# Two decode layers on one core: loading the second layer's first chunks in parts

## The chip, the cores and the metric

The kernel runs on one core of a Trainium2 chip. The metric is the device time of one execution in microseconds (us). It was measured in three runs; the median counts. A further execution was recorded by the hardware profiler.

## The reference, cut to what matters

Two identical layers are applied to four tokens (one per batch entry) of width 512: attention over a cache of 8192 positions, then a SwiGLU feed-forward network (FFN). All data are bfloat16. Both layers use the same weights and the same caches.

```python
# A_x (4,1,512); k_cache, v_cache (4, 8, 8192, 128); wq (512, 4096); wo (4096, 512)
# w_gate, w_up (512, 1792); w_down (1792, 512)
def attention(x):                       # 32 query heads, 8 kv heads, 4 queries for each kv head
    q = (x @ wq) -> (4, 32, 1, 128)
    scores = q . k * 128 ** -0.5
    return (softmax(scores) . v) -> (4, 1, 4096) @ wo

def ffn(x):
    return (silu(x @ w_gate) * (x @ w_up)) @ w_down

for layer in range(2):
    x = x + attention(layernorm(x))
    x = x + ffn(layernorm(x))
```

The K and V caches are 67 MB each and each layer needs both; the weights are some 14 MB.

## The kernel before

**Units and chunks.** A *unit* is one kv head of one batch entry; there are 32 (`unit_order`). The K cache of a unit is a *chunk* of 2 MB, 16 KB for each of the 128 SBUF partitions, and so is its V cache. A chunk has eight blocks of 2 KB per partition, which are the grain of the synchronisation: the resources `s6.0` to `s6.7` are the blocks of slot 6.

**Slots.** SBUF holds eight slots of one chunk each (`NSLOT`). The K and V chunks of layer 1's last three units stay in slots 0 to 5 (`kept`), and layer 2 begins with these three units (29, 30, 31) and goes on with units 0 to 28. So layer 2 loads six chunks fewer. Here *k0* is the kept K chunk of unit 29 and *k1* that of unit 30.

**FFN weights.** They are loaded at the end of each layer into slots 6 and 7 and a stretch behind them. `wg_sb` (w_gate) takes blocks 0 to 6 of slot 6; the last of the four row blocks of w_up (`wu_sb[FR]`) takes block 7 of slot 6 and the beginning of slot 7; w_down follows in slot 7. The other three row blocks of w_up have a place of their own. `at_w` lists the resources that the FFN's matmuls read.

**Loads.** All loads are issued by SP, in the order of the list `items`. `pump()` walks through the list as long as a slot is free; `finished()` frees a slot when the scores (K) or the weighted sum (V) of a unit have been written out, and calls `pump()`. `T.dma` (line 93 issues it) makes SP wait first until all readers of the destination's resources are done (line 63), so SP stands still at a load whose place is still being read, and everything behind it waits too. The 16 DMA engines work through what SP has issued.

At the boundary between the layers, the first K chunk goes to slot 6 and the second to slot 7; `pump()` at the end of `ffn` issues both. The first waits for the matmuls of w_gate and w_up, since both lie in slot 6, the second for those of w_down. The third chunk (a V chunk, `half_it`) takes k0's slot in two halves: `half(0)` after block 3 of k0 has been used, `half(1)` after block 7. The fourth takes k1's slot when k1 is done. From there on chunks take the slots of V 29, K 31, V 30 and so on.

**Compute.** DVE transposes each K block (line 394), PE computes its scores (line 414), DVE, ACT and PE make the softmax (lines 420 to 450), PE multiplies by V (line 495) and, for each four units, by wo (line 522). The kept K chunks are already transposed. The FFN's matmuls are on line 593 (w_gate, then w_up) and 610 (w_down, in three parts). The order of the work on each engine is the order in which the Python program emits it; `keys`, `values`, `line` and `drain` interleave the stages by fixed costs.

Of the kernel before, what the change touches and what calls it, by code (L numbers as in the profile page):

```python
# [103 lines left out]
def bass_interleave_layers__gqa_block_cached__swiglu_ffn__decode_kernel(  # L104
# [12 lines left out]
    B, _, D = A_x.shape  # L117
    _, G, S, Dh = A_k_cache.shape
    HqDh = A_wq.shape[1]
    Hq = HqDh // Dh  # L120
    F = B_w_gate.shape[1]
    REP = Hq // G
    P = 128
    assert Dh == P and B * Hq == P and D % P == 0 and F % P == 0 and B == 4
    KT = D // P
    FO = F // P
    XB = KT * B
    TT = S // P
    TB = 8
    NB = TT // TB  # L130
# [7 lines left out]
    NQ = 4  # L138
    NSLOT = 8
    NKEEP = 6  # L140
# [5 lines left out]
    with ExitStack() as es:  # L146
# [3 lines left out]
        SL = TT * Dh  # L150
        FR = KT - 1
        kvf = sb("kvf", [P, NSLOT * SL + FR * F], BF16)
        kv = kvf[:, 0:NSLOT * SL].rearrange("p (s w) -> p s w", s=NSLOT)
        f0 = NKEEP * SL
        wg_sb = kvf[:, f0:f0 + KT * F].rearrange("p (k f) -> p k f", k=KT)
        wu_sb = [kvf[:, NSLOT * SL + k * F:NSLOT * SL + (k + 1) * F] for k in range(FR)]
        wu_sb.append(kvf[:, f0 + KT * F:f0 + (KT + 1) * F])
        f1 = f0 + (KT + 1) * F
# [1 line left out]
        wd_sb = kvf[:, f1:f1 + FO * D].rearrange("p (f n) -> p f n", f=FO)  # L160
        places = [f"s{s}.{q}" for s in range(NKEEP, NSLOT) for q in range(NB)]
        room = lambda a, b: places[(a - f0) // (TB * Dh):(b - 1 - f0) // (TB * Dh) + 1]
        at_w = {"wg": room(f0, f0 + KT * F) + ["wg"], "wu": room(f0 + KT * F, f1) + ["wu", "wu3"],
                "wd": room(f1, f1 + FO * D)}
        WD = ((0, 6), (6, 12), (12, 14))
        wq_sb = sb("wq_sb", [P, KT, HqDh], BF16)
        wo_sb = sb("wo_sb", [P, Hq, D], BF16)
# [34 lines left out]
        n = 2 * FO * B  # L202
# [10 lines left out]
        def bank_bf(k):  # L213
# [6 lines left out]
        sem = lambda name: es.enter_context(nc.semaphore(name))  # L220
        engines = {"pe": nc.tensor, "act": nc.scalar, "dve": nc.vector, "pool": nc.gpsimd, "sp": nc.sync}
        prog = {n: sem(f"prog_{n}") for n in engines}
        sem_s = [sem(f"sem_s{i}") for i in range(NSLOT)]
        sem_l = [sem(f"sem_l{q}") for q in range(NQ)]
        sem_x = sem("sem_x")
        sem_w = {n: [sem(f"sem_{n}{i}") for i in range(c)]
                 for n, c in (("wq", KT), ("wo", 4), ("wg", 1), ("wu", 2), ("wd", 3))}
        sem_out = sem("sem_out")
        es.enter_context(nc.Block())
        T = _Sync(engines, prog)  # L230
# [25 lines left out]
        def unit_gb(u):  # L256
            return u // B, u % B
# [3 lines left out]
        unit_order = [list(range(NU)), list(range(NU - NRES, NU)) + list(range(NU - NRES))]  # L261
# [10 lines left out]
        items = []  # L272
# [5 lines left out]
        ends = [i for i, it in enumerate(items) if it[0] == "wd"]  # L278
        split = {items[e - 3] for e in ends}

        half_it = items[ends[0] + 3]
        halves = []
        issued = [0]
        free = list(range(NSLOT))
        slot_of = {}
# [1 line left out]
        def load_weight(name, i=0):  # L287
            if name == "wq":
                T.dma("sp", wq_sb[:, i, :], A_wq[i * P:(i + 1) * P, :], sem_w["wq"][i], writes=[f"wq{i}"])
            elif name == "wo":  # L290
                n = Hq // 4
                T.dma("sp", wo_sb[:, i * n:(i + 1) * n, :],
                      A_wo[i * n * Dh:(i + 1) * n * Dh, :].rearrange("(h p) n -> p h n", p=P),
                      sem_w["wo"][i], writes=[f"wo{i}"])
            elif name == "wg":
                T.dma("sp", wg_sb, B_w_gate.rearrange("(kt p) f -> p kt f", p=P), sem_w["wg"][0], writes=places + ["wg"])
            elif name == "wu":
                if i == 0:
                    T.dma("sp", kvf[:, NSLOT * SL:].rearrange("p (k f) -> p k f", k=FR),
                          B_w_up[0:FR * P, :].rearrange("(kt p) f -> p kt f", p=P), sem_w["wu"][0], writes=["wu"])  # L300
                T.dma("sp", wu_sb[FR], B_w_up[FR * P:, :], sem_w["wu"][1], writes=["wu3"])
            else:

                for j, (a, b) in enumerate(WD):
                    T.dma("sp", wd_sb[:, a:b, :].rearrange("p (m e) n -> p m (e n)", e=2),
                          B_w_down[a * P:b * P, :].rearrange("(m p e) n -> p m (e n)", p=P, e=2), sem_w["wd"][j],
                          writes=[f"wd{j}"])

        def pump():
            while issued[0] < len(items):  # L310
                n = issued[0]
                it = items[n]
                if it[0][0] == "w":
                    if it[0] == "wg":
                        if not {NKEEP, NKEEP + 1} <= set(free):
                            return
                        free[:] = [s for s in free if s < NKEEP]
                    load_weight(*it)
                    issued[0] += 1
                    continue  # L320

                late = any(e - 10 < n < e for e in ends)
                fit = [s for s in free if s < NKEEP or not late]
                if not fit:
                    return
                s = fit[0] if late else max(fit, key=lambda s: s >= NKEEP)
                free.remove(s)
                kind, L, u = it
                slot_of[it] = s
                g, b = unit_gb(u)  # L330
                cache = A_k_cache if kind == "K" else A_v_cache
                src = cache[b, g, :, :].rearrange("(p t) d -> p (t d)", p=P)
                if it in split:
                    w = TT * Dh // NQ
                    n8 = NB // NQ
                    for q in range(NQ):
                        T.dma("sp", kv[:, s, q * w:(q + 1) * w], src[:, q * w:(q + 1) * w], sem_l[q],
                              writes=[f"s{s}.{q * n8 + k}" for k in range(n8)])
                else:
                    T.dma("sp", kv[:, s, :], src, sem_s[s], writes=[f"s{s}.{q}" for q in range(NB)])  # L340
                issued[0] += 1

        def half(i):
            kind, L, u = half_it
            g, b = unit_gb(u)
            s = slot_of[half_it]
            w = SL // 2
            src = (A_k_cache if kind == "K" else A_v_cache)[b, g, :, :].rearrange("(p t) d -> p (t d)", p=P)
            T.dma("sp", kv[:, s, i * w:(i + 1) * w], src[:, i * w:(i + 1) * w], sem_l[i],
                  writes=[f"s{s}.{i * NB // 2 + k}" for k in range(NB // 2)])  # L350

        def half_done(it):
            if it == ("K", 1, unit_order[1][0]):
                assert items[issued[0]] == half_it and it in slot_of
                slot_of[half_it] = slot_of[it]
                issued[0] += 1
                half(0)

        def finished(it):
            kind, L, u = it  # L360
            if (kind, 1, u) in kept and L == 0:
                slot_of[kind, 1, u] = slot_of[it]
                if kind == "K":
                    turned.update((1, u, q) for q in range(NB))
            elif it == ("K", 1, unit_order[1][0]):
                half(1)
                pump()
            else:
                free.append(slot_of[it])
                pump()  # L370

# [92 lines left out]
        def keys(L, u):  # L464
            def block(q):
                if q == 0:
                    place_q(u)
                scores(L, u, q)
                if q == NB // 2 - 1:
                    half_done(("K", L, u))  # L470
                if q == NB - 1:
                    finished(("K", L, u))
                    for gap, fn in ((0.0, max_p), (1.0, max_t), (0.9, exps), (1.0, turn_p), (0.3, total)):
                        line.append([gap, u, lambda fn=fn: fn(u)])

            for q in range(NB):
                if (L, u, q) not in turned:
                    turn(L, u, q)
                blocks.append((0.65, lambda q=q: block(q)))
                drain(LAG)  # L480
# [100 lines left out]
        def ffn(last):  # L581
# [5 lines left out]
            for (w_sb, wname, bk) in (([wg_sb[:, k, :] for k in range(KT)], "wg", gb), (wu_sb, "wu", ub)):  # L587
                for fo in range(FO):
                    if bk == gb and fo == FO // 2:
                        deviation(zero_sb, "zero")  # L590
                    f = fo // 2 * 2 * P + fo % 2
                    for kt in range(KT):
                        T.op("pe", lambda e: e.matmul(bank(bk)[:, fo * B:(fo + 1) * B],
                                                      lhsT=w_sb[kt][:, f:f + 2 * P - 1:2],
                                                      rhs=xn[:, kt * B:(kt + 1) * B],
                                                      start=(kt == 0), stop=(kt == KT - 1)),
                             reads=at_w[wname] + ["xn"], writes=[f"pb{bk}"], sig=(fo == FO - 1 and kt == KT - 1))
            T.op("dve", lambda e: e.tensor_tensor(fb(gr), fb(gT), rb, ALU.mult),
                 reads=[f"pb{gb}", "rstd"], writes=["gr"])
            T.op("act", lambda e: e.activation(eg, gr, ACTF.Exp, scale=-1.0), reads=["gr"], writes=["eg"])  # L600
# [6 lines left out]
            for j, (a, b) in enumerate(WD):  # L607
# [6 lines left out]
                             reads=["hT", f"wd{j}"] + at_w["wd"], writes=[f"pb{dn[j]}"], sig=(fo == b - 1))  # L614
                if j < len(WD) - 1:
                    add_to_x(dn[j])
            free.extend((NKEEP, NKEEP + 1))
            pump()
            if last:
                T.op("dve", lambda e: e.tensor_tensor(xoT[:], xT[:], bank(dn[-1])[:, 0:XB], ALU.add),  # L620
# [72 lines left out]
```

## Time and profile before

| | us |
|---|---|
| median of three runs | 668.08 |
| lowest and highest | 667.45, 668.77 |
| the profiled execution | 667.48 |
| its span on the engines | 665.2 |
| PE busy | 495.9 (75%) |
| DVE busy | 380.9 (57%) |
| DMA queue q1, share of 16 engines | 98.4% |
| moved | 274.96 MB, mean 413 GB/s |

All times in the profile count from the start of the span. A "releaser" is the instruction or DMA that ended a wait. The chain is found by going back from the last instruction to what released each one. Busy shares are averages over stages with different limits.

### The profile page before, as it was taken

The page shows a single profiled execution, that of the slowest core. Times are in us where ns is not written, and L with a number is a line of the kernel's source. Part 1 is how long each engine was busy: PE and PEld are TensorE (multiplying, and loading weights), DVE is VectorE, ACT ScalarE, POOL GpSimd, SP SyncE. Part 2 cuts the span into 40 slices and gives each one's busy share as a digit, 9 for nine tenths or more (in the row PEclk, how much of TensorE's full clock was granted, in tenths as well). Part 3 has the DMA queues.
Part 4 walks back from the last instruction along what each step waited for, and adds up shares of the span by engine and source line. Part 5 has one row for each costly group of instructions (what it writes and reads, how often), then busy time and mean ns, then how long its engine had stood idle before and what let it go on. Part 6 is the DMA issues. An engine that isn't in the chain of part 4 may idle for free.

```text
span 665.2 us, 16774 instructions
## 1 busy us (share of the span) xinstructions
PE 495.9 (75%) x7400; PEld 396.5 (60%) x7400; DVE 380.9 (57%) x879; ACT 89.9 (14%) x331; POOL 19.8 (3%) x75
## 2 busy tenths in 40 slices
PE   1765777877867857876775999877777786887686
PEld 1554565655745646665565878755665565665575
DVE  1645565655765655665641279675566465576572
ACT  1010111101101101111110112110110111110120
POOL 0000000000000000000000000000000000000000
PEclk9887788687878788788885979877878868788885
DMA  8999999999999999999998999999999999999996
GB/s 358 416 408 407 420 429 424 426 426 429 425 427 425 427 429 424 428 422 428 427 404 341 345 426 428 426 425 426 429 424 429 426 427 426 424 429 426 426 415 234
DMA packets 27032, 274.96 MB, mean 413 GB/s; under 512 B 2376, under 2 KB 6480, under 8 KB 10960
## 3 DMA queue, kind: packets, MB, share of 16 engines
q1 hardware_dynamic: 26960, 273.89, 98.4%
q8 instruction: 58, 0.95, 0.6%
q14 instruction: 14, 0.11, 0.0%
HBM read 273.88 MB, written 0.00 MB: 412 GB/s over the span
## 4 chain that ended last, share of the span: by engine, by line
DMA 68%; PE 16%; SPq 10%; DVE 3%; issue 2%; POOL 0%; ACT 0%; DVEq 0%; POOLq 0%
DMA kvf<-in_A_k_cache_dram 63%; PE ps L414 11%; SPq L93 10%; DMA kvf<-in_B_w_down_dram 5%; PE ps L495 3%; DVE kvf L394 1%; PE ps L436 1%; PE ps L424 1%; DVE pT L445 0%; PE ps L560 0%; DVE mx L420 0%; PE ps L448 0%; PE ps L610 0%; DVE rl L450 0%; PE ps L574 0%
## 5 line engine op out<-in xcount | busy, mean ns | idle before, releaser
L394 DVE STREAM_TRANSPOSE kvf<-kvf 128x512 f32<-128x512 f32 x488 | 313.2, 677 | 199.4 <-DMA kvf<-in_A_k_cache_dram 199.4
L414 PE MATMUL ps<-kvf,zq 128*128 128x256 bf16 x2048 | 330.6, 318 | 9.5 <-DVE kvf L394 6.5
L414 PEld LDWEIGHTS ps<-kvf,zq 128*128 128x128 bf16 x2048 | 215.3, 113 | 69.7 <-DVE kvf L394 9.8
L495 PE MATMUL ps<-pT,kvf 128*128 128x32 bf16 x4096 | 124.1, 179 | 37.1 <-DVE rl L450 35.1
L495 PEld LDWEIGHTS ps<-pT,kvf 128*128 128x128 bf16 x4096 | 120.8, 97 | 45.1 <-issue 39.8
L424 PE MATMUL ps<-identf,mx 128*1 128x128 f32 x64 | 19.5, 304 | 92.8 <-DVE mx L420 92.8
L430 ACT ACTIVATE pb<-m 1x128 f32<-1x128 f32 x64 | 19.7, 308 | 399.6 <-DVE m L427 399.6
L424 PEld LDWEIGHTS ps<-identf,mx 128*1 128x1 f32 x64 | 5.2, 81 | 96.7 <-DVE mx L420 96.6
L405 POOL TENSOR_TENSOR zq<-scr,quad 128x64 bf16<-128x64 bf16 x64 | 18.7, 292 | 618.3 <-PE ps L414 550.8
L436 PEld LDWEIGHTS ps<-onesf,pb 1*128 1x128 f32 x128 | 24.4, 237 | 19.6 <-issue 17.9
L445 DVE STREAM_TRANSPOSE pT<-pb 128x256 bf16<-128x256 bf16 x64 | 26.9, 421 | 12.6 <-ACT pb L440 12.0
L440 ACT ACTIVATE pb<-ps,nm 128x256 bf16<-128x256 f32 x64 | 30.4, 475 | 2.1
L420 DVE TENSOR_REDUCE mx<-ps 128x1 f32<-128x256 f32 x64 | 25.1, 393 | 8.6 <-PE ps L414 8.6
L436 PE MATMUL ps<-onesf,pb 1*128 1x1 f32 x128 | 29.9, 300 | 0.1
L439 ACT ACTIVATE nm<-ps 128x1 f32<-128x1 f32 x64 | 11.0, 171 | 134.3 <-PE ps L436 134.3
L448 PEld LDWEIGHTS ps<-rsm,onesf 128*128 128x128 f32 x128 | 20.7, 203 | 2.6 <-ACT rsm L442 0.6
L448 PE MATMUL ps<-rsm,onesf 128*128 128x4 f32 x128 | 19.8, 225 | 0.5 <-ACT rsm L442 0.5
L427 DVE TENSOR_REDUCE m<-ps 1x4 f32<-1x128 f32 x64 | 15.9, 249 | 7.1 <-PE ps L424 6.6
L442 ACT ACTIVATE rsm<-head,rs 128x4 f32<-128x4 f32 x64 | 19.0, 297 | 2.1
L503 DVE TENSOR_TENSOR oT<-ps,rl 128x4 bf16<-128x4 f32 x64 | 7.9, 123 | 10.4 <-PE ps L495 10.1
L560 PE MATMUL ps<-xn,wq_sb 128*128 128x4 bf16 x256 | 7.5, 165 | 8.1 <-DMA wq_sb<-in_A_wq_dram 8.1
L522 PEld LDWEIGHTS ps<-oT,wo_sb 128*128 128x128 bf16 x256 | 8.8, 105 | 6.8 <-DVE oT L503 5.2
(55 smaller groups left out, 91.4 us busy)
## 6 DMA issues: line engine op xcount, KB each, us to landing
kvf<-in_A_k_cache_dram SPq DMA_DIRECT2D x61, 2048.0 KB, 31.0
kvf<-in_A_v_cache_dram SPq DMA_DIRECT2D x58, 2048.0 KB, 32.2
wq_sb<-in_A_wq_dram SPq DMA_DIRECT2D x4, 1024.0 KB, 8.1
wo_sb<-in_A_wo_dram SPq DMA_DIRECT2D x4, 1024.0 KB, 19.4
kvf<-in_A_v_cache_dram SPq DMA_DIRECT2D x8, 512.0 KB, 18.8
kvf<-in_B_w_gate_dram SPq DMA_DIRECT2D x2, 1792.0 KB, 23.4
kvf<-in_B_w_down_dram SPq DMA_DIRECT2D x4, 768.0 KB, 16.4
kvf<-in_A_v_cache_dram SPq DMA_DIRECT2D x2, 1024.0 KB, 7.2
```

The costliest lines, as they stand in the source:

```text
L93: ins = self.eng[engname].dma_start(out_ap, in_ap)
L394: T.op("dve", lambda e: e.transpose(w, w), reads=[f"s{s}.{q}"], writes=[f"s{s}.{q}"])
L414: T.op("pe", lambda e: e.matmul(bank(bk)[:, 0:SW], lhsT=zq[:, c, z0:z0 + P], rhs=w[:, :, c // 2, :, c % 2], start=(q == 0 and c == 0), sto ...
L420: T.op("dve", lambda e: e.tensor_reduce(mx[:], bank(bk)[:, 0:SW], AX.X, ALU.max), reads=[f"pb{bk}"], writes=["mx"])
L424: T.op("pe", lambda e: e.matmul(bank(STEP)[0:1, 0:P], lhsT=mx[:], rhs=identf[:], is_transpose=True, start=True, stop=True), reads=["mx", " ...
L430: T.op("act", lambda e: e.activation(mrow.rearrange("p (x h) -> p x h", h=REP), m4[:].unsqueeze(1).to_broadcast([1, QB, REP]), ACTF.Copy), ...
L436: T.op("pe", lambda e: e.matmul(bank(STEP)[:, 0:1], lhsT=mrow, rhs=onesf[0:1, :], start=True, stop=True), reads=["pb", "onesf"], writes=[f ...
L440: T.op("act", lambda e: e.activation(pb[:], bank(bk)[:, 0:SW], ACTF.Exp, bias=nm[:], accum_out=rs[:]), reads=[f"pb{bk}", "nm"], writes=["p ...
L442: T.op("act", lambda e: e.activation(rsm[:], head[:], ACTF.Copy, scale=rs[:]), reads=["head", "rs"], writes=["rsm"])
L445: T.op("dve", lambda e: e.transpose(pT[:, turn_of[u], 0:SW], pb[:]), reads=["pb"], writes=[f"pT{turn_of[u]}"])
L448: T.op("pe", lambda e: e.matmul(bank(TOT)[:, 0:REP], lhsT=ones, rhs=rsm[:], start=True, stop=True), reads=["rsm", "onesf"], writes=[f"pb{T ...
L495: T.op("pe", lambda e: e.matmul(bank(bk)[:, 0:WIDE], lhsT=kv[:, s, t * Dh:(t + 1) * Dh], rhs=pT[:, turn_of[u], c0:c0 + WIDE], start=(t == ...
```

## The change

The first chunk of layer 2 (slot 6) loads in two parts: blocks 0 to 6 once w_gate's matmuls are emitted, block 7 once w_up's are. The third chunk loads in four quarters, after blocks 1, 3, 5 and 7 of k0, and the fourth in two halves, after blocks 3 and 7 of k1. The second is as before. Each part has a semaphore of its own (`sem_p`). In layer 1 alone, the last row block of w_up is loaded by five DMAs of 8, 4, 2, 2 and 112 rows in the place of one of 128 rows. `load` replaces `half` and the issuing code in `pump`; `load_part` replaces `half_done`.

```diff
--- before.py
+++ after.py
@@ -160,8 +160,9 @@
         wd_sb = kvf[:, f1:f1 + FO * D].rearrange("p (f n) -> p f n", f=FO)
         places = [f"s{s}.{q}" for s in range(NKEEP, NSLOT) for q in range(NB)]
         room = lambda a, b: places[(a - f0) // (TB * Dh):(b - 1 - f0) // (TB * Dh) + 1]
-        at_w = {"wg": room(f0, f0 + KT * F) + ["wg"], "wu": room(f0 + KT * F, f1) + ["wu", "wu3"],
+        at_w = {"wg": room(f0, f0 + KT * F) + ["wg"], "wu": room(f0 + KT * F, f1) + ["wu"] + [f"wu3{j}" for j in range(5)],
                 "wd": room(f1, f1 + FO * D)}
+        WU3 = ((0, 8), (8, 12), (12, 14), (14, 16), (16, 128))
         WD = ((0, 6), (6, 12), (12, 14))
         wq_sb = sb("wq_sb", [P, KT, HqDh], BF16)
         wo_sb = sb("wo_sb", [P, Hq, D], BF16)
@@ -222,9 +223,10 @@
         prog = {n: sem(f"prog_{n}") for n in engines}
         sem_s = [sem(f"sem_s{i}") for i in range(NSLOT)]
         sem_l = [sem(f"sem_l{q}") for q in range(NQ)]
+        sem_p = [sem(f"sem_p{i}") for i in range(8)]
         sem_x = sem("sem_x")
         sem_w = {n: [sem(f"sem_{n}{i}") for i in range(c)]
-                 for n, c in (("wq", KT), ("wo", 4), ("wg", 1), ("wu", 2), ("wd", 3))}
+                 for n, c in (("wq", KT), ("wo", 4), ("wg", 1), ("wu", 6), ("wd", 3))}
         sem_out = sem("sem_out")
         es.enter_context(nc.Block())
         T = _Sync(engines, prog)
@@ -278,8 +280,14 @@
         ends = [i for i, it in enumerate(items) if it[0] == "wd"]
         split = {items[e - 3] for e in ends}
 
-        half_it = items[ends[0] + 3]
-        halves = []
+
+        parts = {}
+        k0, k1 = (("K", 1, u) for u in unit_order[1][:2])
+        for it, ps_ in ((items[ends[0] + 1], (("wg", 0, 7), ("wu", 7, 8))),
+                        (items[ends[0] + 3], [((k0, q + 1), q, q + 2) for q in range(0, NB, 2)]),
+                        (items[ends[0] + 4], [((k1, q + 3), q, q + 4) for q in range(0, NB, 4)])):
+            for ev, a, b in ps_:
+                parts[ev] = (it, a, b, sem_p[len(parts)])
         issued = [0]
         free = list(range(NSLOT))
         slot_of = {}
@@ -298,7 +306,9 @@
                 if i == 0:
                     T.dma("sp", kvf[:, NSLOT * SL:].rearrange("p (k f) -> p k f", k=FR),
                           B_w_up[0:FR * P, :].rearrange("(kt p) f -> p kt f", p=P), sem_w["wu"][0], writes=["wu"])
-                T.dma("sp", wu_sb[FR], B_w_up[FR * P:, :], sem_w["wu"][1], writes=["wu3"])
+                for j, (a, b) in enumerate(WU3 if i == 0 else ((0, P),)):
+                    T.dma("sp", wu_sb[FR][a:b], B_w_up[FR * P + a:FR * P + b, :], sem_w["wu"][1 + j],
+                          writes=[f"wu3{j}"])
             else:
 
                 for j, (a, b) in enumerate(WD):
@@ -327,34 +337,29 @@
                 free.remove(s)
                 kind, L, u = it
                 slot_of[it] = s
-                g, b = unit_gb(u)
-                cache = A_k_cache if kind == "K" else A_v_cache
-                src = cache[b, g, :, :].rearrange("(p t) d -> p (t d)", p=P)
                 if it in split:
-                    w = TT * Dh // NQ
                     n8 = NB // NQ
                     for q in range(NQ):
-                        T.dma("sp", kv[:, s, q * w:(q + 1) * w], src[:, q * w:(q + 1) * w], sem_l[q],
-                              writes=[f"s{s}.{q * n8 + k}" for k in range(n8)])
+                        load(it, q * n8, (q + 1) * n8, sem_l[q])
                 else:
-                    T.dma("sp", kv[:, s, :], src, sem_s[s], writes=[f"s{s}.{q}" for q in range(NB)])
+                    load(it, 0, NB, sem_s[s])
                 issued[0] += 1
 
-        def half(i):
-            kind, L, u = half_it
-            g, b = unit_gb(u)
-            s = slot_of[half_it]
-            w = SL // 2
-            src = (A_k_cache if kind == "K" else A_v_cache)[b, g, :, :].rearrange("(p t) d -> p (t d)", p=P)
-            T.dma("sp", kv[:, s, i * w:(i + 1) * w], src[:, i * w:(i + 1) * w], sem_l[i],
-                  writes=[f"s{s}.{i * NB // 2 + k}" for k in range(NB // 2)])
-
-        def half_done(it):
-            if it == ("K", 1, unit_order[1][0]):
-                assert items[issued[0]] == half_it and it in slot_of
-                slot_of[half_it] = slot_of[it]
-                issued[0] += 1
-                half(0)
+        def load(it, a, b, sm):
+            kind, L, u = it
+            s = slot_of[it]
+            w = TB * Dh
+            src = (A_k_cache if kind == "K" else A_v_cache)[u % B, u // B, :, :].rearrange("(p t) d -> p (t d)", p=P)
+            T.dma("sp", kv[:, s, a * w:b * w], src[:, a * w:b * w], sm, writes=[f"s{s}.{q}" for q in range(a, b)])
+
+        def load_part(ev, s):
+            if ev in parts:
+                it, a, b, sm = parts.pop(ev)
+                if a == 0:
+                    assert items[issued[0]] == it
+                    slot_of[it] = s
+                    issued[0] += 1
+                load(it, a, b, sm)
 
         def finished(it):
             kind, L, u = it
@@ -362,10 +367,7 @@
                 slot_of[kind, 1, u] = slot_of[it]
                 if kind == "K":
                     turned.update((1, u, q) for q in range(NB))
-            elif it == ("K", 1, unit_order[1][0]):
-                half(1)
-                pump()
-            else:
+            elif it not in (k0, k1):
                 free.append(slot_of[it])
                 pump()
 
@@ -466,8 +468,8 @@
                 if q == 0:
                     place_q(u)
                 scores(L, u, q)
-                if q == NB // 2 - 1:
-                    half_done(("K", L, u))
+                it = ("K", L, u)
+                load_part((it, q), slot_of[it])
                 if q == NB - 1:
                     finished(("K", L, u))
                     for gap, fn in ((0.0, max_p), (1.0, max_t), (0.9, exps), (1.0, turn_p), (0.3, total)):
@@ -595,6 +597,7 @@
                                                       rhs=xn[:, kt * B:(kt + 1) * B],
                                                       start=(kt == 0), stop=(kt == KT - 1)),
                              reads=at_w[wname] + ["xn"], writes=[f"pb{bk}"], sig=(fo == FO - 1 and kt == KT - 1))
+                load_part(wname, NKEEP)
             T.op("dve", lambda e: e.tensor_tensor(fb(gr), fb(gT), rb, ALU.mult),
                  reads=[f"pb{gb}", "rstd"], writes=["gr"])
             T.op("act", lambda e: e.activation(eg, gr, ACTF.Exp, scale=-1.0), reads=["gr"], writes=["eg"])
@@ -614,7 +617,7 @@
                              reads=["hT", f"wd{j}"] + at_w["wd"], writes=[f"pb{dn[j]}"], sig=(fo == b - 1))
                 if j < len(WD) - 1:
                     add_to_x(dn[j])
-            free.extend((NKEEP, NKEEP + 1))
+            free.append(NKEEP + 1)
             pump()
             if last:
                 T.op("dve", lambda e: e.tensor_tensor(xoT[:], xT[:], bank(dn[-1])[:, 0:XB], ALU.add),
```

## The prediction

> **What bounds the kernel now.** I read the page's slices first. Its rows are TensorE's granted clock, the DMA engines' share, and what they moved, in 40 slices of 16.6 us.
>
> ```profile
> DMA  8999999999999999999998999999999999999996
> GB/s 358 416 408 407 420 429 424 426 426 429 425 427 425 427 429 424 428 422 428 427 404 341 345 426 428 426 425 426 429 424 429 426 427 426 424 429 426 426 415 234
> ```
>
> The kernel streams at 424 to 429 GB/s nearly throughout: it is bound by DMA. The one dip inside is slices 21 to 23 (404, 341, 345), the boundary between the layers. The windows view divides it (time, length, busy us of PE, PEld, DVE, ACT, POOL, clock, DMA share, GB/s):
>
> ```profile
> 345.00:351.00 6.00, 2.98 (x65) 2.71 (x65) 1.13 (x7) 0.00 (x0) 0.00 (x0) 0.50 1.04 401
> 351.00:357.40 6.40, 3.32 (x109) 3.09 (x109) 1.73 (x7) 0.81 (x3) 0.00 (x0) 0.50 0.69 244
> 357.40:367.00 9.60, 6.30 (x85) 4.91 (x86) 1.53 (x9) 0.56 (x2) 0.29 (x1) 0.51 0.97 406
> 367.00:369.00 2.00, 1.87 (x17) 1.37 (x15) 0.09 (x1) 0.00 (x0) 0.00 (x0) 1.00 0.77 201
> 369.00:374.00 5.00, 4.63 (x53) 3.91 (x54) 1.44 (x5) 1.34 (x5) 0.38 (x2) 1.00 0.93 329
> 374.00:376.00 2.00, 2.00 (x63) 1.89 (x60) 0.67 (x3) 0.31 (x1) 0.20 (x1) 1.00 1.05 295
> 376.00:385.00 9.00, 8.63 (x225) 7.71 (x222) 2.08 (x6) 1.34 (x5) 0.00 (x0) 0.94 0.97 405
> 385.00:395.00 10.00, 8.89 (x114) 6.99 (x111) 8.56 (x19) 1.34 (x5) 0.58 (x2) 0.71 1.01 429
> ```
>
> Against 428 GB/s these rows lose 0.38 + 2.75 + 0.49 + 1.06 + 1.16 + 0.62 + 0.48 = 6.9 us, the most that refilling the dip could be worth. Next, SP's timeline, which says when each load was allowed:
>
> ```profile
> 340.46 5.63 SPq L93 DMA_DIRECT2D kvf<-in_B_w_down_dram  x3
> 356.00 3.43 SPq L93 DMA_DIRECT2D kvf<-in_A_k_cache_dram  x2
> 367.18 2.10 SPq L93 DMA_DIRECT2D kvf<-in_A_v_cache_dram  x2
> 373.84 0.33 SPq L93 DMA_DIRECT2D kvf<-in_A_k_cache_dram  x1
> 375.55 0.33 SPq L93 DMA_DIRECT2D kvf<-in_A_v_cache_dram  x1
> 379.67 0.33 SPq L93 DMA_DIRECT2D kvf<-in_A_k_cache_dram  x1
> 381.37 0.33 SPq L93 DMA_DIRECT2D kvf<-in_A_v_cache_dram  x1
> 392.58 0.33 SPq L93 DMA_DIRECT2D kvf<-in_A_k_cache_dram  x1
> ```
>
> Between 356 and 381 SP issues seven chunks (the two V entries at 367 are halves of one). Then it waits until 392.58: all eight slots are full or in use, and the next comes free when the scores of unit 0 are done. The chain in order of time says what sets that moment and when DMA takes over again:
>
> ```profile
> 391.15 1.36 PE ps L414 x12
> 392.88 1.01 DVE kvf L394 x2
> ...
> 403.48 0.66 DVE kvf L394
> 404.23 18.47 DMA kvf<-in_A_k_cache_dram
> ```
>
> From 358.7 (end of the FFN) to 404 the chain is PE and DVE, without a wait for data. So 392.58 follows from the FFN's end plus 34 us of compute, and earlier loads do not move it.
>
> **Sixteen engines, not one.** The trace also keeps, for each DMA, when each of its 16 engines signalled. In layer 1 the spread of these marks grows from 0.75 us (18 us in) to 7.1, one engine at a time in steps of 1.55 us, roughly once per packet of the page's queue "q8 instruction: 58". At w_down's last piece seven engines signal at 351.8 to 353.0 and nine at 356.0 to 358.65. So the dip is mostly the seven prompt engines idling. They are not the ones that end the kernel: at the last w_down piece of layer 2 the marks again spread over 6.2 us (655.65 to 661.84), and the latest releases the last matmuls.
>
> **The change part by part.**
>
> *K chunk in slot 6, 7/8 after w_gate, 1/8 after w_up.* Now all of it goes at 356.00, when w_up's last matmul ends. w_gate's last ends at 351.9, so 1792 KB go 4.1 us earlier. For a late engine, busy with weights until 358.65, this changes nothing: issue to first data takes 1.95 us (373.84 to first landing 380.67, less 4.89 for a chunk), so the chunk was waiting for it already. A prompt engine idles from 351.8 to about 353.9 instead of 358.0.
>
> *V chunk in four quarters, K chunk in halves.* The quarters are released after blocks 1, 3, 5, 7 of kept unit k0 (about 365.4, 367.2, 368.0, 368.9 from PE's rows), the K halves after blocks 3 and 7 of k1 (371.4, 373.8). The last K half therefore has data from 373.84 + 1.95 = 375.8 and is in at 378.3, where the whole chunk now lands at 380.67 on the promptest engine: 2.4 us earlier for those without a penalty on the way.
>
> *Where that goes.* Three more chunks follow (375.55, 379.67, 381.37 are already issued by then): 378.3 + 3 x 4.89 = 393.0. The next chunk cannot have data before 392.58 + 1.95 = 394.5. Before, these engines finished the same chunk at 395.33. So of 2.4 us an engine without a penalty keeps 395.33 - 394.5 = **0.8 us**, and 1.5 become a new idle stretch at 393. A late engine gets more: the marks of that chunk spread from 395.33 to 398.24, six of them over 1.2 late. The 1.5 us of slack absorb one penalty of 1.55, so these gain 0.8 + 1.55, or **2.4 us**. The end is set by whichever engine is last at 661; some ten take penalties, and the four latest there lie within 0.8 us, so if one of them was late at 395 the next takes its place. I take **1.5 us**, just under the middle.
>
> *Smaller transfers.* Rows get shorter: 4 KB for V, 2 KB for the eighth. The nearest rows are the four 512 KB quarters that end layer 1: 407 to 415 GB/s (330 to 340 us) against 426, 3 to 5%; on 4 MB (9.8 us) 0.3 to 0.5 us, hidden in the 1.5 us of new idle. From below nothing: shorter rows save no bytes. [...]
>
> *w_up's last quarter in five pieces (layer 1 only).* Four more issues at 0.33 to 0.43 us, up to 1.7 us of SP's time near 340; w_down's pieces are queued behind. They are issued by 346.1, and the promptest engine needs the last at about 351, so this is covered by 3 us; uncovered it would cost 1.7. PE waits for four more semaphores before w_up's matmuls, 0.04 each as "issue" in the chain: 0 to 0.2. The marks do not name engines, so shifting rows between them is bounded by two rows of 3,584 B (0.14 us each) either way: -0.3 to +0.3, taken as 0. [...]
>
> *FFN's end.* Prompt engines now move K while late ones still bring w_down. The spread shrank from 7.1 to 6.8 while the prompt ones stood idle; without that help 0 to 0.3 us on the end, which moves 392.58 as well. Taken as 0.
>
> PE, ACT, DVE and POOL keep the same instructions in the same order; only SP's list changes. SP's waits stand in the order of their releases, so nothing is held behind a later one.
>
> **Sum.** 667.48 (span 665.2 and 2.3 around it) - 1.5 = 666.0 for the profiled execution. The median of three runs is 0.6 above it: 668.08 - 1.5 = **666.6**.
>
> **Rivals.**
> - *The dip is refilled in full.* All 6.9 us come back, or the late engines turn out to idle more than I read: 4 to 6.9 us, 661 to 664. For: the GB/s rows. Against: eight slots and 392.58. Chance 0.12.
> - *Nothing reaches the end.* The latest engine at 661 took all its penalties after 395 and extra idle eats its 0.8: 667.5 to 668.4. Chance 0.08.
> - *Slower: the five-piece w_up delays the FFN.* Its main piece has 112 rows from partition 16 on, seven per engine and askew to the others' eight. If its share (7 x 0.14 = 1 us) takes three times as long, or w_down's issues lose their cover, the FFN ends 2 to 3 us later, and 392.58 with it, since that is compute after the FFN. From 0.8 us on this eats the gain; 2.2 us and more are slower by over 1.3: 669.4 to 670.3. For: the late engines have no idle before 358.65, so any delay shows. Against: SP's 3 us of cover. Chance 0.18.
> - *My forecast*, 0.8 to 2.4 gained, 665.7 to 667.3: chance 0.62. How the 1.55 us penalties fall on engines can move the last one by half a step either way.
>
> **How the numbers follow.** A change under 0.2% (1.3 us) is about what a measurement of this kernel can tell from none. Of my forecast two thirds of the way from 0.8 to 2.4 lie beyond it (0.40), the rest within (0.22). Faster 0.40 + 0.12 = 0.52; same 0.22 + 0.08 = 0.30; slower 0.18. The range 665.0 to 669.0 holds the forecast with half a step, the second rival, and the mild part of the slower one; it leaves out the full refill and a strong slow-down. The forecast's own range is 665.2 to 667.6.
>
> **What would show it.** Right: GB/s near 428 at 357 to 376, a new dip just before 394.5, SP's issue still near 392.6, and the span shorter by far less than 6.9. Wrong: SP's issue after 381 well before 392 (the cap was not compute), or L610's last matmuls later than 358.9 (the slower rival).

## The result and the profile after

The changed kernel is slower: a median of 670.2 us over eight runs (668.36 to 671.75) against 668.25 over eight runs of the kernel before; the ratio is 1.0029 [1.0016, 1.0043], some 2 us. The profiled execution is the longest of its eight, 671.75 with a span of 669.6, against 667.48 and 665.2 before. So its trace has 4.3 us to explain, about twice the usual loss.

The page's slices, as before (DMA engines' busy share in tenths, and what they moved):

```profile
DMA  8999999999999999999999899999999999999995
GB/s 358 415 411 405 420 430 424 426 427 427 424 430 421 430 427 424 429 423 429 422 371 347 309 401 426 427 428 425 427 423 430 425 426 427 428 424 426 427 414 215
```

The dip at the layer boundary is not refilled. It is four slices long in the place of three: 371, 347, 309, 401 where 404, 341, 345, 426 stood. The windows view (time, length, busy us of PE, PEld, DVE, ACT, POOL, clock, DMA share, GB/s) divides it with the bounds used before:

```profile
345.00:351.00 6.00, 1.87 (x34) 1.59 (x34) 1.13 (x7) 0.00 (x0) 0.00 (x0) 0.50 1.04 311
351.00:357.40 6.40, 2.74 (x83) 2.69 (x84) 1.35 (x5) 0.81 (x3) 0.00 (x0) 0.50 1.02 321
357.40:367.00 9.60, 5.69 (x134) 4.90 (x132) 1.92 (x11) 0.56 (x2) 0.29 (x1) 0.50 0.93 362
367.00:369.00 2.00, 2.00 (x12) 1.33 (x10) 0.00 (x0) 0.00 (x0) 0.00 (x0) 0.50 0.75 299
369.00:374.00 5.00, 4.50 (x28) 3.14 (x27) 0.42 (x1) 0.00 (x0) 0.29 (x1) 0.71 0.86 277
374.00:376.00 2.00, 2.00 (x18) 1.59 (x17) 0.28 (x1) 0.84 (x3) 0.00 (x0) 1.00 0.88 297
376.00:385.00 9.00, 9.00 (x188) 8.11 (x186) 3.31 (x10) 1.92 (x9) 0.29 (x1) 1.00 0.94 342
385.00:395.00 10.00, 8.11 (x148) 6.21 (x146) 5.59 (x11) 1.26 (x5) 0.29 (x1) 0.70 1.00 426
395.00:405.00 10.00, 10.00 (x188) 8.91 (x187) 8.70 (x20) 1.61 (x6) 0.58 (x2) 0.96 0.95 382
```

The kernel before in the last of these windows (the prediction shows the others):

```profile
395.00:405.00 10.00, 10.00 (x171) 8.73 (x170) 10.00 (x23) 2.38 (x9) 0.58 (x2) 1.00 1.01 426
```

Three things are to be seen. In the first two rows the DMA engines are fully busy (1.04, 1.02) and move 311 and 321 GB/s: busy and slow for 12 us. Before, only the row of 2 us from 374 was like that (1.05, 295). In 351 to 357.4 this is still more than the 244 of before, and than the 249 of the five pieces alone (e2 below), so the early K part does fill idle time. And in 367 to 369 the clock is 0.50 where it was 1.00. Summed over 345 to 405, rows times lengths, 21.13 MB were moved where before it was 22.70: 1.57 MB less, at 428 GB/s 3.7 us. At w_down's last piece in layer 2 the marks of the first engine stand at 659.16 (655.65 before) and of the last at 666.21 (661.84), 3.5 and 4.4 later. So nearly all of the loss is there by 405.

SP's timeline, when loads were issued:

```profile
340.45 9.47 SPq L93 DMA_DIRECT2D kvf<-in_B_w_down_dram  x3
353.20 8.62 SPq L93 DMA_DIRECT2D kvf<-in_A_k_cache_dram  x3
367.98 4.97 SPq L93 DMA_DIRECT2D kvf<-in_A_v_cache_dram  x4
...
397.12 0.33 SPq L93 DMA_DIRECT2D kvf<-in_A_k_cache_dram  x1
```

w_down's pieces are issued when they were before (340.45; 340.46), so SP was not the cause. The first K part goes 2.8 us earlier (353.20; 356.00). But the chunk that waits for a slot goes at 397.12 in the place of 392.58, 4.5 us late. The chain in order of time says what those 4.5 us are:

```profile
360.44 0.93 PE ps L613 x29
...
366.01 6.54 PE ps L416 x32
...
397.12 0.30 issue
...
408.77 17.54 DMA kvf<-in_A_k_cache_dram
```

The same two stretches in the kernel before:

```profile
358.06 0.93 PE ps L610 x29
...
363.63 5.25 PE ps L414 x32
```

The FFN ends at 361.4 (359.0 before): **2.4 us**. The scores of k0, the 32 matmuls of the second line, took 6.5 us where they took 5.25. The clock's own record has it at half speed until 371.9 here and until 366.8 before; from the FFN's end to the issue it is 35.7 us, where it was 33.6: **2.1 us**. DMA takes over the chain at 408.77, where it did at 404.23.

### The profile page after: what moved, and what is told of

It is laid out like the page before. It is cut to its first block, busy times and chain, and to the rows that moved or that the text cites. A ratio compares the mean times of both kernels' runs of the same rounds, so it can differ in the third digit from the quotient of the medians.

```text
span 669.6 us, 16788 instructions
## 1 busy us (share of the span) xinstructions
PE 495.2 (74%) x7400; PEld 394.4 (59%) x7400; DVE 380.8 (57%) x879; ACT 89.9 (13%) x331; POOL 19.9 (3%) x75
## 4 chain that ended last, share of the span: by engine, by line
DMA 68%; PE 16%; SPq 10%; DVE 3%; issue 2%; POOL 0%; ACT 0%; DVEq 0%; POOLq 0%
DMA kvf<-in_A_k_cache_dram 63%; PE ps L416 10%; SPq L93 10%; DMA kvf<-in_B_w_down_dram 5%; PE ps L497 3%; DVE kvf L396 1%; PE ps L438 1%; PE ps L426 1%; DVE pT L447 0%; PE ps L562 0%; DVE mx L422 0%; PE ps L450 0%; PE ps L613 0%; DVE rl L452 0%; POOL zq L407 0%
## 5 line engine op out<-in xcount | busy, mean ns | idle before, releaser
L447 DVE STREAM_TRANSPOSE pT<-pb 128x256 bf16<-128x256 bf16 x64 | 26.9, 421 | 13.5 <-ACT pb L442 13.1
```

What stands on the lines that cost most here:

```text
L447: T.op("dve", lambda e: e.transpose(pT[:, turn_of[u], 0:SW], pb[:]), reads=["pb"], writes=[f"pT{turn_of[u]}"])
```

## The experiments

Two theories stood first. In A the five pieces of w_up are the cost and the parts are harmless, or bring what I had forecast. In its rival the parts are the cost, by setting K data beside w_down's last pieces. Kernels with an edit to "before" are marked so; line numbers move a little with the edits.

**Each half of the change alone.** `e1_parts_only`, edit to the changed kernel:

```diff
-        WU3 = ((0, 8), (8, 12), (12, 14), (14, 16), (16, 128))
+        WU3 = ((0, 128),)
```

> The change without the five pieces: w_up's last row block moves in one DMA of 128 rows in both layers; the part loads stay. Theory A (the five pieces slow every DMA packet while they are in the queues and so delay the FFN's end): w_up's last landing is back near 354.2 us, the FFN ends near 359, SP's issue after 381 is near 392.6, and the median is 0.8 to 2.4 us below the kernel before, 665.7 to 667.3. Theory B (the K part that starts while late engines still bring weights is what delays them): w_up and w_down still land 2 us late and the median is 1 to 3 us above the kernel before.

667.97 against 668.08, ratio 0.9998 [0.9989, 1.0008]. The loss is gone: w_down's last mark is at 358.68 (358.66 before), with a K part issued at 351.80 flowing beside it. So the parts do not slow the FFN. But there is no gain either: the next chunk is issued at 393.40, the clock having come back at 368.0, and it lands on the first engine at 400.49, where the kernel before had 400.40.

`e2_five_only`, edit to before (with `WU3` as in the change, and the names and semaphores of the pieces, not shown):

```diff
...
-                T.dma("sp", wu_sb[FR], B_w_up[FR * P:, :], sem_w["wu"][1], writes=["wu3"])
+                for j, (a, b) in enumerate(WU3 if i == 0 else ((0, P),)):
+                    T.dma("sp", wu_sb[FR][a:b], B_w_up[FR * P + a:FR * P + b, :], sem_w["wu"][1 + j],
+                          writes=[f"wu3{j}"])
```

> The kernel before with the five pieces of w_up's last row block in layer 1 and nothing else. Theory A: packets of 3,584 B take over 200 ns instead of 142 in the stretch where the pieces move, w_gate's last landing comes 1 us and w_down's 2 us late, the FFN ends near 361, and the median is 2 to 4 us above the kernel before. Theory B: the stretch is as before and the median within 0.5 us of it.

670.03, ratio 1.0033 [1.0021, 1.0046]: the whole loss. w_down's last mark is at 360.70, 2.0 late, the clock returns at 371.4 and the next chunk goes at 396.35. The DMA view of this kernel from 335 to 362 us, in 40 slices of 0.675 us, shows how:

```profile
DMA  9999999999999999999999999988765555399589
GB/s 431 388 413 369 413 460 374 400 383 429 416 404 388 413 400 398 356 238 240 247 248 357 404 404 342 300 221 233 261 191 195 215 228 228 149 209 267 185 340 388
```

Slices 18 to 21 (346.5 to 349.2) are the finding: the engines are busy throughout and the rate is 240 GB/s, little over half of the 400 on either side. Those are the times at which the prompt engines reach the five pieces. The second dip mixes two things, the late engines reaching the same pieces at 352 to 354 and the prompt ones standing idle (shares of 5 to 8). The trace's single packets agree: 3,584-byte packets, of w_up's neighbours too, took 235 ns from 346 to 348 and 217 from 352 to 354 (medians), against 144 and 140 in the kernel before. So it is not the pieces alone that are slow but what is in flight with them.

**What about the pieces does it?** `e3_two_16_112` and `e4_two_8_120`, edits to before, replace the one DMA by two, by rows. Here e3; e4 has `((0, 8), (8, 128))`:

```diff
+        WU3 = ((0, 16), (16, 128))
...
-                T.dma("sp", wu_sb[FR], B_w_up[FR * P:, :], sem_w["wu"][1], writes=["wu3"])
+                for j, (a, b) in enumerate(WU3 if i == 0 else ((0, P),)):
+                    T.dma("sp", wu_sb[FR][a:b], B_w_up[FR * P + a:FR * P + b, :], sem_w["wu"][1 + j],
+                          writes=[f"wu3{j}"])
```

> The kernel before with w_up's last row block of layer 1 in two pieces, 16 rows (one for each engine) and 112 rows (seven for each). Theory A1 (it is the 112-row piece, whose seven rows per engine lie across the groups of eight that the engines otherwise write): packets slow down as in the changed kernel, over 200 ns for 3,584 B, FFN end about 361. Theory A2 (it is the pieces of 8, 4, 2 and 2 rows, which only some engines carry): packets stay at 142 ns and the FFN ends near 359.

> The kernel before with w_up's last row block of layer 1 in two pieces of 8 and 120 rows. If engines take equal numbers of rows, 120 rows go to fifteen engines of eight rows each, whole groups but shifted by one group. Theory A1 in the form that rows lying across groups are the cause: no slow-down here, 142 ns, FFN end near 359 to 360. In the form that any group other than the engine's own is the cause, or that few engines carry a piece: over 200 ns and an FFN end near 361.

670.14 and 670.48, one run each. Packets of 3,584 bytes took 225 and 245 ns in the two dips with 16 and 112 rows, 243 and 221 with 8 and 120; w_down's last marks are at 361.26 and 361.60, later than with five pieces. So it takes neither the tiny pieces (4, 2, 2 rows) nor five of them, and 120 rows, a multiple of eight, slow the stream as 112 do.

`e5_columns`, edit to before, makes two DMAs of the same size by columns: 128 rows of 1,792 bytes each.

```diff
...
-                T.dma("sp", wu_sb[FR], B_w_up[FR * P:, :], sem_w["wu"][1], writes=["wu3"])
+                for j, (a, b) in enumerate(((0, F // 2), (F // 2, F)) if i == 0 else ((0, F),)):
+                    T.dma("sp", wu_sb[FR][:, a:b], B_w_up[FR * P:, a:b], sem_w["wu"][1 + j], writes=[f"wu3{j}"])
```

> The kernel before with w_up's last row block of layer 1 in two pieces by columns: 128 rows of 1,792 B each, twice. Theory A3 (a transfer that has not all 128 rows gives the engines other partitions than a full one, so they get in each other's way): no slow-down, packets of the neighbours stay at 142 to 145 ns, w_down's last landing near 358.7. Theory A4 (any further DMA or smaller piece at this place costs): neighbours over 200 ns and w_down's landing near 361 as with the pieces by rows.

667.93 in one run, beside 668.09 for the kernel before; neighbouring packets 140 to 144 ns, w_down's last mark at 358.89. The same view as above, of this kernel:

```profile
DMA  9999999999999999999999999755555499589899
GB/s 394 401 407 376 397 413 406 412 405 400 418 405 401 424 380 401 388 410 396 390 404 393 395 377 376 292 203 218 225 231 209 167 237 255 200 364 437 364 437 437
```

The dip at 346.5 is gone; only the idle one from 352 on is left, which the kernel before has too. One more DMA, and half the bytes for each row, cost nothing that can be seen.

**The same on the plain stream.** `e6_cut_chunks` cuts four 2 MB K chunks of layer 1 in two, far from weights and boundary: unit 10 by rows into 16 and 112, unit 14 into 64 and 64, unit 22 into 8 and 120, and unit 18 by columns. Edit to before:

```diff
+        CUT = {("K", 0, 10): (0, ((0, 16, 0, SL), (16, P, 0, SL))), ("K", 0, 14): (1, ((0, 64, 0, SL), (64, P, 0, SL))),
+               ("K", 0, 18): (2, ((0, P, 0, SL // 2), (0, P, SL // 2, SL))), ("K", 0, 22): (3, ((0, 8, 0, SL), (8, P, 0, SL)))}
...
+                    T.dma("sp", kv[r0:r1, s, c0:c1], src[r0:r1, c0:c1], sem_c[j], writes=[f"cut{j}"])
+                    T.dma("sp", kv[r2:r3, s, c2:c3], src[r2:r3, c2:c3], sem_s[s], writes=[f"s{s}.{q}" for q in range(NB)])
...
```

> The kernel before with four K chunks in the middle of layer 1 cut in two: unit 10 by rows 16 + 112, unit 14 by rows 64 + 64, unit 18 by columns 64 + 64, unit 22 by rows 8 + 120. Theory A3: while the pieces by rows move, all packets slow down by half or more and the stream falls to some 300 GB/s for a few us each, 64 + 64 as well, while the cut by columns stays at 426; the median is 3 to 8 us above the kernel before. Theory A4 would show all four. If it were something of the weights' place, none of the four would slow down and the time would stay near 668.

690.79 in one run: 22.7 us more than the kernel before, 7.6 for each of the three chunks cut by rows, far over what any theory expected. First its DMA view from 112 to 139 us (slices of 0.675), around the chunk in 16 and 112 rows, then from 205 to 225 (slices of 0.5), around the one cut by columns:

```profile
DMA  9999899999989998979998998969779999999999
GB/s 437 413 461 413 376 461 388 413 413 194 267 194 243 218 170 146 218 170 267 194 218 194 243 267 170 218 146 243 194 316 437 413 485 437 413 388 388 461 388 437
```
```profile
DMA  9899999999999899999999999999899999999999
GB/s 492 360 426 393 492 459 393 393 393 442 459 410 393 360 426 442 426 410 410 426 410 475 393 442 426 459 442 508 360 393 426 426 524 393 393 393 492 426 459 393
```

In the first, 20 slices (118.1 to 131.6) run at about half of the rate, 209 GB/s in the mean, with the engines mostly at 9. In the second nothing happens. The other two row cuts look like the first: 229 GB/s for 14.9 us (64 and 64) and 222 for 17.4 us (8 and 120). In the three stretches 16 KB packets took 1,160 to 1,206 ns (medians) in the place of 613. Against 426 GB/s they cost 6.9, 6.9 and 8.3 us, together 22.1 of the measured 22.7. A chunk of 2 MB alone would be at half rate for 9.8 us. That the stretches are longer fits the spread of the engines (the chunk ahead of the first cut ends on them between 118.0 and 122.6): those that have passed the cut would still suffer from those that have not. No run tests that.

**Where the parts' gain went.** At its end the kernel before waits for unit 0's slot (the scores of K 0). `e7_swap`, edit to before, has V 31, a kept chunk that needs no load, weighted before the scores of unit 0, so that its slot comes free sooner; the remaining query projection moves with it.

```diff
-            for i, (kind, _, u) in enumerate(work(L)):
-                if L == 1 and (kind, u) == ("K", 0):
+            seq = work(L)
+            if L == 1:
+                v31 = ("V", 1, unit_order[1][NRES - 1])
+                seq.remove(v31)
+                seq.insert(seq.index(("K", 1, 0)), v31)
+            for i, (kind, _, u) in enumerate(seq):
+                if L == 1 and (kind, u) == ("V", unit_order[1][NRES - 1]):
```

> The kernel before with V of unit 31 (kept) used before K of unit 0 in layer 2, and the query projection of the remaining heads ahead of it; loads in the same order. Theory C (between the layers the stream is held by the number of free slots: the next one comes free only when the scores of unit 0 are done, and that moment moves with the granted clock): SP's issue after 381 comes near 387 instead of 392.6, the stream has no gap near 394, and the median is 0 to 1 us below the kernel before. Rival: the order costs compute that ends later, 0 to 1 us above.

667.59, ratio 0.9996 [0.9988, 1.0005]. SP's issue is at 389.77 in the place of 392.58, and the stream flows on without a gap there. But the gap that it closes was small: the chunks on either side landed 5.07 apart before, 4.90 now.

`e8_parts_swap` is e1 with the edit of e7:

> The part loads without the five pieces, and V of unit 31 ahead of K of unit 0 as in the swap alone. Theory C: the part loads bring the seven chunks in by 393 on prompt engines, the next slot is free by 387, so nothing is lost again and the median is 1.5 to 3 us below the kernel before, though the part loads alone gave nothing. Rival (the part loads gain nothing because the late engines set the end): within 0.5 us of the kernel before.

667.40, ratio 0.9989 [0.9980, 0.9998]; the issue is at 390.84 and the chunks land 4.89 apart without a gap. A gain of 0.7 us, not 1.5 to 3. The same kernel again on another chip, `e11_parts_swap_again`:

> The same kernel as the part loads with V of unit 31 first, on one chip with the next one. Its last comparison gave 0.9989 (0.998 to 0.9998). If the idle matmuls add nothing of their own, this one and the next come out within 0.5 us of each other, at 0.7 to 1.5 us below the kernel before.

667.55, ratio 0.9996 [0.9986, 1.0005]. The two intervals overlap; the medians differ from the kernel before by 0.7 and 0.3 us.

**The clock.** `e9_warm`, edit to before, gives PE 34 idle matmuls (128x128 weights, 256 columns; their results are not read) in its gaps from layer 1's FFN to the first scores of layer 2:

```diff
+        def busy(k):
+            for _ in range(k if warm[0] else 0):
+                T.op("pe", lambda e: e.matmul(bank(STEP)[:, 0:SW], lhsT=wq_sb[:, 0, 0:P], rhs=wq_sb[:, 1, 0:SW],
+                                              start=True, stop=True), writes=[f"pb{STEP}"], sig=False)
...
+                busy(8 if bk == gb else 10)
```

> The kernel before with idle matmuls (128x256 into an unused PSUM bank, not part of the result) in PE's gaps from the FFN of layer 1 to the first scores of layer 2, 32 in all. Theory C (the stream's gaps after the boundary are set by compute that runs at half the granted clock for 8 to 10 us after the FFN's end): the clock is back at 1.0 before the first kept unit, that unit takes some 3.5 us instead of 5.2 to 6.5, SP's issue after 381 comes 2 to 3 us earlier, and the median is 0.5 to 2 us below the kernel before. If the gate does not count these matmuls, or the FFN is delayed by them, the clock comes back as late as before and the median is 0 to 1 us above.

667.76, ratio 0.9996 [0.9987, 1.0005]. Its windows:

```profile
345.00:351.00 6.00, 5.16 (x74) 3.66 (x75) 1.13 (x7) 0.00 (x0) 0.00 (x0) 0.50 1.03 399
351.00:357.40 6.40, 5.81 (x122) 4.71 (x122) 1.71 (x7) 0.81 (x3) 0.00 (x0) 0.50 0.78 257
357.40:367.00 9.60, 9.12 (x98) 5.50 (x96) 1.54 (x10) 0.56 (x2) 0.29 (x1) 0.50 0.93 389
```

PE was busy for 5.16 of 6.0, 5.81 of 6.4 and 9.12 of 9.6 us, and the clock stayed at 0.50 until 368.6. So in this execution these matmuls did not hold the clock up, with PE busy for 95% of the third row (by the profile, whose ends of matmuls are modelled). The lengths go in steps: in all traces of this study the half-speed stretch over the layers' boundary lasts 20.5, 23.9 or 27.3 us, 3.4 apart.

`e10_parts_swap_warm`, parts, order and idle matmuls together, and `e12_parts_swap_warm_again`, the same once more:

> Part loads without the five pieces, V of unit 31 first, and the idle matmuls as well. Theory C: nothing gates the stream after the boundary but the slots, and they come free 2 to 3 us earlier, so the median is 1.5 to 4 us below the kernel before. Rival (late engines set the end whatever the boundary does): within 1 us of it.

> The same kernel with the idle matmuls, whose last comparison gave 0.9979 (0.997 to 0.9988), though its profile showed that they do not hold the clock up. If they help all the same, by moving the moment at which the clock comes back, this one is 0.7 to 1.3 us below the one without them; if not, within 0.5 us.

666.43, ratio 0.9979 [0.9970, 0.9988], and 666.44, ratio 0.9974 [0.9964, 0.9985]: 1.5 us less than the kernel before, on two chips, and the best version found. The profiled e10 had the clock back at 366.1 and issued at 388.94; the profiled e12, the longest of its eight at 668.17, at 369.1 and 390.33. The idle matmuls are worth about 1 us here (e10 and e12 against e8 and e11, 666.4 against 667.4 to 667.55) and nothing in e9. Why is open in part: in e11, without them, the clock was back at 366.8 too, and one profile for each kernel does not show how often it returns when.

The clock's record read against PE's rows goes a step further. Count steps of 3.4 us back from the end of the half-speed stretch. In the eleven profiles without idle matmuls, the stretch ends with the first step of which k0's scores fill 78% or more; steps that they filled to less than 73% did not end it. In e10 it ended after a step with 63% of scores, 90% together with idle matmuls; in e9 and e12 steps with 39% and 42%, 81% and 83% together, did not end it. (In the kernel before, a half-speed stretch of one step, 325.9 to 329.3, ended though scores filled 23% of it; V matmuls, line 495, filled 61%. So 78% is a reading of this place and no rule.) So in these profiles the clock's return went with where the steps fell, which differs from one execution to the next (the stretch begins at 342.9 in the kernel before and at 346.3 in e11), and idle matmuls may bring it a step forward in some executions. That this is their 1 us is not shown.

## Why the prediction was wrong

- **The term that failed: the five pieces.** "bounded by two rows of 3,584 B (0.14 us each) either way: -0.3 to +0.3, taken as 0." The bound counted who carries which row, and took each packet's duration as fixed. Measured, the five pieces alone cost 1.95 us in the median (e2), which is the whole loss of the change. The FFN ends 2.0 us (five pieces alone) to 2.4 us later, because the packets in flight beside the pieces of fewer than 128 rows took 1.5 to 1.7 times as long (medians of 217 to 245 ns for 140 to 144). No row of the trace of before could price this, since no large transfer in it has fewer than 128 rows; then the term's ends should have been far apart.
- **The slower rival was what happened.** It had the place (the 112-row piece), the path (late engines have no idle before 358.65, so FFN's end and 392.58 move) and the time, 669.4 to 670.3 for 670.2 measured. Its mechanism was too small: it slowed the piece's own share threefold, while e2 and e6 show the neighbours slowed. So that its time came out is in part luck. Its counter-argument, SP's 3 us of cover, was beside the point: w_down was issued on time. It should have had more than 0.18. The sign given for it, L610 later than 358.9, was misread: in the kernel before the FFN ends at 359.0, not at 358.7.
- **That a cut by rows could cost was not weighed.** The prediction priced smaller transfers by their size. Size is not what bit: e5's two DMAs, by columns, are of 224 KB each and lose nothing (667.93 beside 668.09). Beside the cuts by rows of e6, 16 KB packets went from 613 ns to 1,160 to 1,206, for the neighbours too.
- **"392.58 follows from the FFN's end plus 34 us of compute"**: right in kind. No earlier load moved it in e1 (393.40), and in the changed kernel it moved with the FFN. Wrong in that the 34 us are not fixed. From FFN's end to the issue it took 33.6 us where the clock returned 7.8 us after the FFN's end (before), 34.4 at 9.0 (e1), 35.3 at 10.4 (e2) and 35.7 at 10.5 (changed kernel). An FFN that ends later by 2.4 can miss a step of the clock and lose 2.1 more, as the profiled execution did; e3 and e4, clock back at 369.4, did not (33.6 and 33.3). That the executions of one kernel differ by up to 3.4 us fits such steps: the profiles with the latest return, 371.9 and 371.4, are the longest runs of their kernels.
- **"I take 1.5 us" for the parts: 0.1, with an interval from 0.5 worse to 0.7 better.** The K part did flow early, 351.80 in e1, and the rows 351 to 357.4 rose from 244 to 363 GB/s there. But the sum has the last K half in at 378.3 on the promptest engine, and in e1 it landed at 380.32, only 0.35 before the whole chunk of the kernel before (380.67). It was issued at 374.40 in the place of 373.8, the clock being late, and took 5.92 us to land where the sum had 4.4 (1.95 and 2.45 for 1 MB); why is not shown. Three chunks later the first engine was at 394.95 (395.33 before), and the cap took the rest: issued at 393.40, the next chunk cannot flow before an estimated 395.35. So nearly all of the 2.4 us was missing before the cap came in, and that the result is the second rival's (0.08) is by another way. With the cap moved (e8, e11) the gain is 0.7 and 0.3 us in the medians; that the 1.55 us penalties would add to the gain found no support. The profile of e11 suggests where a gain can stay. Its clock was back when it was in the kernel before, and the K half landed at 379.43, 1.2 earlier; at layer 2's last w_down piece the first engine was at 654.01 (655.65 before), but the last at 661.91 (661.84 before), and the spans are 665.3 and 665.2. There the prompt engines kept their gain and the latest one set the end, as the second rival had it.
- **The full refill** had the right argument against it: eight slots. With the slot freed earlier (e8) it did not come either.

What stays open is why pieces of fewer than 128 rows held the stream at about half its rate (240 GB/s in e2, 209 to 229 in e6). The trace names the engine of neither a packet nor a mark, so which rows an engine carried and which partitions it wrote is not shown; the equal shares and groups of eight in the prediction and in the expectations for e3 and e4 are an assumption. Engines that get in each other's way, as the expectation for e5 has it, would suit all three cuts and the neighbours' delay, but no trace shows it. A cut by rows also changes which rows of DRAM the engines read at one time, and no run separates the two sides.

## What to carry to other kernels

In a stream that is bound by DMA, cut a transfer by columns and leave it all 128 partitions: here a cut by rows took everything in flight from 426 to between 209 and 229 GB/s, for 13.5 to 17.4 us where 2 MB at half rate would take 9.8, and a cut by columns left the stream at 425 (e6, one run). Before loading earlier, find what ends the next wait for a buffer, here the scores of unit 0: until that wait moves, earlier loads only move the idle time. Check also when the last part lands, not only when the parts are issued. And where a trace has no row for the new kind of operation, a term of 0 with a narrow bound says more than is known.

## What the runs showed of the hardware that I had not expected

- Two DMAs of 16 and 112, 64 and 64, or 8 and 120 rows in the place of one of 128 held the stream at 209, 229 and 222 GB/s in the place of 426, with the engines busy, at 7.6 us for each 2 MB (e6, one run). Two of 128 rows by columns left it at 425 (window of 208 to 219 us).
- A busy share of 9 said nothing of the rate: 240 and 430 GB/s both show it (e2, 335 to 349 us). Read the two rows together.
- The granted clock stayed at 0.50 for 9.6 us in which PE was 95% busy (e9), and the stretches at half speed differed by steps of 3.4 us from one trace to the next (20.5, 23.9 and 27.3).
